# Five split units in layer 1 and LayerNorm sums on GpSimd, in a two-layer transformer kernel

## The chip, the cores and the metric

The kernel runs on one core of a Trainium2 chip. The metric is the device time of one execution in microseconds (us): before the change 2511.05 us, the median of three runs (2510.99 to 2511.12).

The core's engines run their own instruction streams and wait for one another on semaphores. In the profile PE is the matrix engine (PEld its weight loads), DVE the vector engine, ACT the scalar engine with its function tables, POOL the GpSimd engine, and SP the queue from which this kernel issues its DMAs. L1701 is line 1701 of the kernel's file.

## The reference

Two identical layers over 2048 tokens of width 512; A is attention with 32 heads of 16, B a gated FFN of width 1792. The weights are the same in both layers.

```python
def _A_ref(x, wqkv, wo):
    qkv = (x @ wqkv).reshape(B, S, 3, H, Dh) ...
    scores = jnp.einsum("bhqd,bhkd->bhqk", q, k) * (Dh ** -0.5)
    p = _softmax(scores, axis=-1)
    o = jnp.einsum("bhqk,bhkd->bhqd", p, v)
    return o ... @ wo
def _B_ref(x, w_gate, w_up, w_down):
    return (_gelu(x @ w_gate) * (x @ w_up)) @ w_down

x = A_x
x = x + _A_ref(_layernorm(x), A_wqkv, A_wo)
x = x + _B_ref(_layernorm(x), B_w_gate, B_w_up, B_w_down)
x = x + _A_ref(_layernorm(x), A_wqkv, A_wo)
x = x + _B_ref(_layernorm(x), B_w_gate, B_w_up, B_w_down)
```

## The kernel before

**Units.** Attention is cut into units: a block of queries (512 in layer 0; 512, 512, 512, 256, 128 and 128 in layer 1) by a group of four heads. Eight groups make 32 units of 512 queries in layer 0. Every unit goes through two passes. In **pass 1** PE computes scores with queries as rows (L1686), and DVE takes their row maximum over 512 keys, one or two score tiles an instruction (L1701, in `p1_emit`). The maxima of the four blocks of keys are joined on POOL (`fin_pool`, L1062 to L1064), transposed on DVE (L1066) and moved by small DMAs into a spare row of the query tile (`negmax`), so that in **pass 2** PE's scores, now with keys as rows (L1556), come out with the maximum taken off. ACT takes the exponential, again one or two tiles at a time (L1532, in `p2_emit`), PE multiplies by V with a column of ones (L1580), and `nrm` (L1152 on ACT, L1162 and L1167 on POOL) divides. Pass 1 runs ahead of pass 2 by at most six units.

**Folds.** When ACT has time, `f_emit` computes the difference of scores of two blocks of keys (queries times KD, a difference of keys that POOL prepares at L1317), ACT takes its Relu (L1512), and one DVE instruction (L1696) adds the other block's scores and takes the maximum, in place of two tiles of L1701. `want_fold` decides by how far pass 1 is ahead.

**The seam.** Layer 1 needs K and V of all tokens, and those come out of layer 0's last FFN block. So the first six units of layer 1 do pass 1 on the first three of four blocks of keys first, and the first `NSPL` = 3 units also do pass 2 in two parts: part 0 over three blocks of keys with the maximum so far (`fin_part`), kept by ACT in an unused column range of the tile ATT (`part_out`, `keep_part`, L1125); part 1 over the last block, once its K is there. `merge` (L1033, L1036, L1041) scales the kept part and `nrm` adds it on POOL (L1156). All first parts stand ahead of all second parts in the order of units. The last unit of the kernel is split too, with its own place.

**The rest.** `outproj` multiplies by WO and adds to the residual X, `ffn` runs LayerNorm, gate with gelu on ACT (L1262), up and down products; between them, `ln_to_xnt` normalises and transposes tiles of 128 tokens. Its statistics come from `ln_head`: bn_stats and bn_aggr on DVE (L784, L786), then on POOL plus epsilon, power -0.5 and minus the mean (L788, L790, L792) and the normalised tile (L796). It is called as ("mid", layer) ahead of the FFN and as ("in", layer) ahead of the next layer's projections, in groups of up to four tiles. A version on POOL, `ln_pool`, is there and off (`LNP` = 0). Projections, FFN products and the like go through one or two of the eight PSUM banks, and results are taken out by ACT mostly (`pick`).

**The order of the work** is written by a planner in Python while the program is built: it keeps an estimated clock of each engine and at each step chooses between pass 1, pass 2, P times V, the chains of other work (generators that yield what they wait for, each with a due time) and filler matmuls (L1725) that keep PE busy. An engine runs its instructions strictly in the planned order. A chain's step on DVE, ACT or POOL is planned as soon as the estimated times of its operands are near, whatever else that engine has queued. 21 constants of the planner are taken from the rows of `PLAN`, one row for every 16 steps of pass 1 (lead times, how far pass 1 may lead, how much other work at once, how many banks for pairs). Its 129 rows cover the 2048 steps.

The weights lie in SBUF for the whole run; WO is loaded once (`ld_late`). HT holds the FFN's inner activations (14 x 512 columns) and has a lock, `locks["HT"]`, and so has the pair of normalised tiles XN.

## Time and profile before

| | |
|---|---|
| runs, median (lowest, highest) | 2511.05 us (2510.99, 2511.12) |
| the profiled execution: time, span of its instructions | 2511.16 us, 2509.4 us |
| granted TensorE clock | 1.000 |
| busy: PE, DVE, ACT, POOL | 2436.2, 2410.5, 2347.2, 723.2 us |
| row maximum on DVE (L1701), exponential on ACT (L1532) | 2218.8, 2005.3 us |
| bn_stats and bn_aggr of X on DVE (L784, L786) | 47 of each |
| kept first parts (L1125) | 4 |

A group row of the profile reads: line, engine, operation, written tile <- read tiles, shapes, count | busy us, mean ns of one | idle us of the engine just ahead of them, and what ended it. A row of a stretch of time reads: from:to, length, busy us of PE, PEld, DVE, ACT and POOL (with counts), the granted clock, the DMA share and GB/s. A row of the timeline reads: start, us, engine, line, operation. Operations on DVE and ACT overlap a little, so a count times a mean can be above the busy time.

### The profile page before, as it was taken

To read this page: it belongs to the slowest core of one execution; us is meant where nothing else is said; L and a number is where in the kernel's file an instruction comes from. 1 tells how busy PE (TensorE), PEld (TensorE's weight loads), DVE (VectorE), ACT (ScalarE), POOL (GpSimd) and SP (SyncE) were. 2 spreads that over 40 slices of the span, in tenths; PEclk is the share of its full clock that TensorE was granted. 3 is DMA by queue.
4 is the path that set the end of the run, shared out by engine and by line. 5 is a ranking of instruction groups with operands and counts; after the bars stand their busy time and mean duration, and the time that the engine had idled before them with its cause. 6 is when DMAs were issued, how large, how long until landed. Compare 5 with 4: busy or idle time off the path is not lost.

```text
span 2509.4 us, 69489 instructions
## 1 busy us (share of the span) xinstructions
PE 2436.2 (97%) x30346; PEld 1171.7 (47%) x30346; DVE 2410.5 (96%) x3201; ACT 2347.2 (94%) x3293; POOL 723.2 (29%) x1205
## 2 busy tenths in 40 slices
PE   8999999999999999999999999999999999999999
PEld 3444443544444344444434455434553445544655
DVE  8999999999999999999999999999999999999994
ACT  6999999999999999899988699999999999989987
POOL 4112133222312244241144211241213411343431
PEclk9999999999999999999999999999999999999999
DMA  3110000000000000000000000000000000000000
GB/s 95 45 57 6 4 9 2 2 2 9 4 2 2 4 4 6 4 6 2 10 20 2 12 2 2 8 2 10 3 5 6 5 8 2 3 4 11 5 3 11
DMA packets 28225, 25.16 MB, mean 10 GB/s; under 512 B 10768, under 2 KB 26896, under 8 KB 27920
## 3 DMA queue, kind: packets, MB, share of 16 engines
q1 hardware_dynamic: 27920, 20.71, 2.9%
q8 instruction: 238, 3.90, 0.6%
q14 instruction: 67, 0.55, 0.1%
HBM read 9.70 MB, written 2.10 MB: 5 GB/s over the span
## 4 chain that ended last, share of the span: by engine, by line
PE 49%; ACT 31%; DVE 20%; issue 1%; POOL 0%; ACTq 0%; POOLq 0%
ACT SCR L1532 27%; DVE PM L1701 18%; PE PS L1686 16%; PE PS L688 13%; PE PS L1580 11%; PE PS L1556 4%; PE PS L1725 4%; ACT SCR L1512 1%; DVE SCR L1696 1%; PE PS L1505 0%; ACT KT L560 0%; PE PS L850 0%; ACT AO L1180 0%; ACT ATTT L705 0%; ACT XNT L705 0%
## 5 line engine op out<-in xcount | busy, mean ns | idle before, releaser
L1701 DVE TENSOR_REDUCE PM<-PS 128x2 f32<-128x1024 f32 (+1 forms) x2536 | 2218.8, 934 | 51.8 <-PE PS L1556 16.9
L1532 ACT ACTIVATE SCR<-PS 128x1024 bf16<-128x1024 f32 (+1 forms) x2557 | 2005.3, 900 | 58.1 <-PE PS L1556 42.5
L1686 PE MATMUL PS<-KT,QT 32*128 32x512 bf16 x3911 | 1027.7, 385 | 40.2 <-DVE PM L1701 26.5
L1556 PE MATMUL PS<-QT,KT 32*128 32x512 bf16 (+2 forms) x5120 | 916.5, 340 | 3.5 <-ACT SCR L1532 2.6
L1580 PE MATMUL PS<-VP,SCR 128*128 128x51 bf16 (+1 forms) x16384 | 812.4, 188 | 12.5 <-ACT SCR L1532 7.6
L1580 PEld LDWEIGHTS PS<-VP,SCR 128*128 128x128 bf16 x16384 | 574.2, 96 | 491.2 <-issue 406.5
L1686 PEld LDWEIGHTS PS<-KT,QT 32*128 32x128 bf16 x3911 | 245.8, 91 | 526.4 <-DVE PM L1701 290.2
L1725 PE MATMUL PS<-WV,ZER 128*128 128x240 bf16 x2362 | 426.8, 266 | 2.7 <-ACT SCR L1532 2.0
L1162 POOL TENSOR_TENSOR RL<-ACCS,CM 128x16 f32<-128x16 f32 (+2 forms) x71 | 182.7, 2574 | 606.3 <-ACT ACCS L1152 605.6
L1556 PEld LDWEIGHTS PS<-QT,KT 32*128 32x128 bf16 x5120 | 246.9, 91 | 69.5 <-ACT SCR L1532 42.8
L1725 PEld LDWEIGHTS PS<-WV,ZER 128*128 128x128 bf16 x2362 | 177.1, 96 | 66.2 <-issue 52.9
L1280 POOL TENSOR_TENSOR HT<-HT,AO 128x512 bf16<-128x512 bf16 (+1 forms) x106 | 120.9, 1142 | 194.2 <-ACT AO L1278 194.2
L1317 POOL TENSOR_TENSOR KD<-KT 128x512 bf16<-128x512 bf16 x80 | 92.1, 1153 | 220.1 <-PE PS L1505 187.9
L1062 POOL TENSOR_TENSOR PM<-PM 128x16 f32<-128x16 f32 (+3 forms) x146 | 33.3, 228 | 422.7 <-DVE PM L1701 406.9
L688 PE MATMUL PS<-XNT,WU 128*128 128x512 bf16 (+2 forms) x504 | 135.2, 357 | 0.2 <-DVE PM L1696 0.2
L688 PE MATMUL PS<-WD,HT 128*128 128x512 bf16 x448 | 130.3, 380 | 0.0
L1696 DVE CUSTOM_DVE_ANT_0 SCR<-PS,SCR 128x512 bf16<-128x512 f32 x185 | 119.0, 686 | 3.2 <-PE PS L1686 1.0
L688 PE MATMUL PS<-XNT,WG 128*128 128x512 bf16 (+2 forms) x504 | 119.2, 358 | 0.2
L1512 ACT ACTIVATE SCR<-PS 128x512 bf16<-128x512 f32 (+1 forms) x126 | 103.8, 824 | 15.4 <-PE PS L1505 15.1
L1262 ACT ACTIVATE HT<-PS 128x512 bf16<-128x512 f32 (+2 forms) x126 | 68.6, 550 | 38.0 <-PE PS L688 37.5
L1182 POOL TENSOR_TENSOR X<-X,AO 128x512 f32<-128x512 f32 x46 | 58.3, 1268 | 146.8 <-ACT AO L1180 146.8
L1278 ACT ACTIVATE AO<-PS 128x512 f32<-128x512 f32 (+1 forms) x106 | 64.5, 610 | 0.2
(106 smaller groups left out, 1001.0 us busy)
## 6 DMA issues: line engine op xcount, KB each, us to landing
KT<-SG SPq DMA_DIRECT2D x64, 64.0 KB
QT<-MT SPq DMA_DIRECT2D x236, 1.0 KB
...
QT<-MT SPq DMA_DIRECT2D x68, 0.2 KB
```

The costliest lines, as they stand in the source:

```text
L688: ins = e.matmul(out_ap, lhsT=l, rhs=r_, start=(i == 0), stop=(i == n - 1))
L1162: emit("pool", lambda e: e.tensor_tensor(RL[:, s, 0:4 * nq], lsum, CM1[:, 0:4 * nq], op=ALU.pow), r=[("ACCS", s), ("CM1",)], w=[("RL", s)] ...
L1280: emit("pool", lambda e, ft=ft, o=o: e.tensor_tensor(HT[:, ft, c0:c0 + n], HT[:, ft, c0:c0 + n], AO[:, o, 0:n], op=ALU.mult), r=[("AO", o) ...
L1317: emit("pool", lambda e: e.tensor_tensor(KD[:, s, :], KT[:, g, ka * 512:(ka + 1) * 512], KT[:, g, kb * 512:(kb + 1) * 512], op=ALU.subtrac ...
L1512: emit("act", lambda e: e.activation(PT[:, s0:s0 + cnt, :], PS[:, bk:bk + cnt, :], ACTF.Relu), r=bks, w=[("PT", s0 + d) for d in range(cnt ...
L1532: emit("act", lambda e: e.activation(dst, src, ACTF.Exp, scale=DH ** -0.5), r=[BK[bk + i] for i in range(cnt)], w=[("PT", i) for i in slot ...
L1556: ins = e.matmul(bank(bk)[:, i * n:(i + 1) * n], lhsT=KT[32 * j:32 * j + 32, g, kt * 128:(kt + 1) * 128], rhs=QT[32 * j:32 * j + 32, s, 0: ...
L1580: ins = e.matmul(acc, lhsT=PT[:, slot, i * n + qt * 128:i * n + (qt + 1) * 128], rhs=AP(VP, (kt * H + 4 * g + j) * 17, [[NTT * H * 17, 128 ...
L1686: ins = e.matmul(bank(b), lhsT=QT[32 * j:32 * j + 32, s, qt * 128:(qt + 1) * 128], rhs=KT[32 * j:32 * j + 32, g, kb * 512:(kb + 1) * 512], ...
L1696: emit("dve", lambda e, i=i, b=b, sl=sl: e.tensor_tensor_reduce(PT[:, sl, :], bank(b), PT[:, sl, :], 1.0, -3.0e38, ALU.add, ALU.max, po[:, ...
L1701: emit("dve", lambda e: e.tensor_reduce(po, PS[:, bs[0]:bs[0] + cnt, :], axis=AX.X, op=ALU.max), r=bks, w=[("PM", sm) + h[1:] for h in hs] ...
L1725: return e.matmul(PS[:, b, NACC:512], lhsT=ZER[:, :], rhs=WV[:, 0, 0:512 - NACC], start=(b != 7), stop=(b != 7), skip_group_check=True)
```

## The change

- `NSPL` goes from 3 to 5: units 3 and 4 of layer 1 are also done in two parts. Their first parts are kept in the tile of the output weight WO, as 2 x 272 fp32 columns. So part 0 of these two may not begin before layer 0's output projections are all done (`p2_group`), WO is loaded again from memory when both have been merged (`wo_again`), and layer 1's projections wait for that. The last unit's helper slots are shared with unit 0 (`split[u] % NSPL`).
- `ln_pool` is rewritten and takes 20 tiles from `ln_head`: the first eight tiles of ("mid", 0) and of ("in", 1), and the first four of ("mid", 1). It works on four tiles at once: sum by halving in fp32, minus mean, centre, square, sum by halving, power, then the four normalised tiles. Its workspace is eight rows of HT, so that the ("in", 1) groups take HT's lock.
- Room is made: the constant -1 has one column, the statistics one slot, and there is one helper slot less.
- `XL` = 1000 lets `evac` choose DVE when pass 1 leads by over 1000 steps, which the six units don't allow.
- 114 of the 129 rows of `PLAN` are replaced by 117 others, so there are 132; rows behind the 129th are past the last step of pass 1.

```diff
@@ -24,129 +24,132 @@
-    (0.3, 0.1, 0.55, 0.0, 0.0, -0.05, 2, 0, 14, 84, 8, 40, 0.3, 1.0, 0, 2, 2, 2, 5, 2, 0.0),
+    (0.2, 0.1, 0.55, 0.42, 0.3, -0.05, 2, 0, 30, 84, 8, 60, 0.3, 2.0, -5, 2, 4, 3, 7, 1, -0.05),
     (0.2, 0.1, 0.65, 0.62, 0.3, -0.05, 1, 2, 30, 84, 8, 60, 0.3, 1.5, -5, 2, 4, 3, 9, 4, -0.05),
-    (0.3, 0.1, 0.55, 0.42, 0.0, 0.05, 2, 0, 30, 84, 8, 40, 0.3, 2.0, 0, 2, 2, 2, 5, 2, 0.0),
     (0.2, 0.1, 0.55, 0.62, 0.3, -0.05, 1, 2, 30, 84, 8, 60, 0.3, 2.0, -5, 2, 4, 3, 9, 1, -0.05),
-    (0.1, 0.1, 0.55, 0.62, 0.3, -0.05, 1, 2, 30, 84, 8, 60, 0.3, 2.0, -5, 2, 4, 3, 9, 2, -0.05),
...
+    (0.35, 0.1, 0.75, 0.52, 0.3, -0.05, 3, 0, 5, 10, -30, 80, 0.3, 1.5, -5, 2, 1, 3, 5, 1, 0.2),
     (0.1, 0.05, 0.55, 0.42, 0.3, -0.05, 1, 1, 30, 100, 8, 40, 0.5, 2.0, 10, 14, 1, 2, 11, 3, -0.1),
 ]
...
-           NSPL=3, LNP=0, LNT=12
+           NSPL=5, LNT=8, XL=1000
@@ -344,7 +347,7 @@
-        CM1 = sb("CM1", [128, 16], F32)
+        CM1 = sb("CM1", [128, 1], F32)
@@ -359,14 +362,13 @@
-        ST = sb("ST", [128, 4, 6], F32)
+        ST = sb("ST", [128, 1, 6], F32)
-        NSB = NSPL + 1
+        NSB = NSPL
-        LS = sb("LS", [128, 512], F32) if LNP else None
@@ -375,7 +377,7 @@
-        dma_groups = ["ldw_q", "ldw_k", "ldw_v", "ldw_o", "ldw_g", "ldw_u", "ldw_d"]
+        dma_groups = ["ldw_q", "ldw_k", "ldw_v", "ldw_o", "ldw_g", "ldw_u", "ldw_d", "ldw_o2"]
@@ -387,6 +389,8 @@
+        for i in range(3, NSPL):
+            sch.add_alias(("WOP", i - 3), ("WO",))
@@ -699,7 +703,7 @@
-            if pick() == "dve":
+            if fast and pos["p1"] - pos["p2"] > XL or pick() == "dve":
...
@@ -729,61 +733,62 @@
-        def ln_sum(i, xa, xk, first, col, dur):
...
-        def ln_pool(tts, x_of, ready, at):
...
+        def ln_pool(tts, x_of, ready, at, own):
+            n = len(tts)
+            lk = [("HT", r) for r in range(2 * n)]
+            xk = [x_of(tt)[1] for tt in tts]
+            lv = HT[:, 0:2 * n, :].rearrange("p a b -> p (a b)").bitcast(F32).rearrange("p (a b) -> p a b", a=n)
+            xv = X[:, tts[0]:tts[0] + n, :]
+            def tree(w):
+                while w:
+                    yield ("pool", [], [])
+                    emit("pool", lambda e, w=w: e.tensor_tensor(lv[:, :, 0:w], lv[:, :, 0:w], lv[:, :, w:2 * w], op=ALU.add),
+                         r=lk, w=lk, dur=0.18 + n * w / 520.0)
+                    w //= 2
+            for tt in tts:
+                yield ("cond", lambda tt=tt: ready(tt))
+            h = D // 2
+            yield ("pool", xk, lk)
+            emit("pool", lambda e: e.tensor_tensor(lv[:, :, 0:h], xv[:, :, 0:h], xv[:, :, h:D], op=ALU.add),
+                 r=xk, w=lk, dur=0.18 + n * h / 520.0)
+            yield from tree(h // 2)
+            yield ("pool", [], [("LNS", i) for i in range(n)])
+            emit("pool", lambda e: e.tensor_scalar(LNS[:, 2, 0:n], lv[:, :, 0], -1.0 / D, None, op0=ALU.mult),
+                 r=lk, w=[("LNS", i) for i in range(n)], dur=0.24)
+            for i, tt in enumerate(tts):
+                yield ("pool", [], [])
+                emit("pool", lambda e, i=i, tt=tt: e.tensor_scalar(lv[:, i, :], X[:, tt, :], 1.0, LNS[:, 2, i:i + 1], op0=ALU.mult, op1=ALU.add),
+                     r=[xk[i], ("LNS", i)], w=lk[2 * i:2 * i + 2], dur=0.77)
+                yield ("pool", [], [])
+                emit("pool", lambda e, i=i: e.tensor_tensor(lv[:, i, :], lv[:, i, :], lv[:, i, :], op=ALU.mult),
+                     r=lk[2 * i:2 * i + 2], w=lk[2 * i:2 * i + 2], dur=0.18 + D / 520.0)
+            yield from tree(h)
+            yield ("pool", [], [])
+            emit("pool", lambda e: e.tensor_scalar(LNS[:, 0, 0:n], lv[:, :, 0], 1.0 / D, LN_EPS, op0=ALU.mult, op1=ALU.add),
+                 r=lk + [("LNS", i) for i in range(n)], w=[("LNS", i) for i in range(n)], dur=0.24)
+            emit("pool", lambda e: e.tensor_tensor(LNS[:, 1, 0:n], LNS[:, 0, 0:n], CM05[:, 0:n], op=ALU.pow),
+                 r=[("LNS", i) for i in range(n)] + [("CM05",)], w=[("LNS", i) for i in range(n)], dur=0.59 + 0.16 * (n - 1))
+            if not own:
+                locks["HT"] = False
+            for i, tt in enumerate(tts):
+                xa, xki = x_of(tt)
+                yield ("cond", lambda i=i: at["tr"] > i - 2)
+                yield ("pool", [xki, ("LNS", i)], [("XN", i % 2)])
+                emit("pool", lambda e, i=i, xa=xa: e.tensor_scalar(
+                    XN[:, i % 2, :], xa, LNS[:, 2, i:i + 1], LNS[:, 1, i:i + 1], op0=ALU.add, op1=ALU.mult),
+                    r=[xki, ("LNS", i)], w=[("XN", i % 2)], dur=0.77)
+                at["xn"] = i
...
@@ -866,14 +871,18 @@
                                    XNT[:, :, tt * 128:(tt + 1) * 128], [("XNT", tt)])
                     xnt_rec[tt] = tag
                 return
+            by_pool = tag != ("in", 0) and not fast and tts[0] < (LNT - 4 if tag == ("mid", NL - 1) else LNT)
+            if by_pool and tag[0] == "in":
+                yield ("cond", lambda: ready(tts[-1]) and not locks.get("HT") and not locks.get("XN"))
+                locks["HT"] = True
             while locks.get("XN"):
                 yield ("cond", lambda: not locks.get("XN"))
             locks["XN"] = True
-            by_pool = LNP and tag != ("in", 0) and not fast and (tag == ("mid", NL - 1) or tts[0] < LNT)
             if tag == ("in", 0):
                 add(ln_fast(tts, x_of, ready, at, 0.3), due)
             else:
-                add((ln_fast if fast else ln_pool if by_pool else ln_head)(tts, x_of, ready, at), due)
+                own = tag[0] == "mid"
+                add(ln_fast(tts, x_of, ready, at) if fast else ln_pool(tts, x_of, ready, at, own) if by_pool else ln_head(tts, x_of, ready, at), due)
             for i, tt in enumerate(tts):
                 yield ("cond", lambda i=i: at["xn"] >= i)
                 yield ("pe", [("XN", i % 2)], [("XNT", tt)])
...
@@ -997,7 +1006,7 @@
-            i = split[u]
+            i = split[u] % NSPL
...
@@ -1115,6 +1124,9 @@
             i = split[u]
             if i == NSPL:
                 return ATT[:, 2:2 + units[u][3] // 128, 0:136].bitcast(F32), [("ATTX",)]
+            if i >= 3:
+                return (WO[:, :, :].rearrange("p a b -> p (a b)").bitcast(F32)[:, (i - 3) * NACC:(i - 2) * NACC].rearrange("p (a b) -> p a b", a=4),
+                        [("WOP", i - 3)])
             lo = (0, 192, 328)[i]
             return (ATT[:, :, lo:lo + 136].bitcast(F32),
                     [("ATT", g) for g in range(lo // 64, (lo + 135) // 64 + 1)])
@@ -1159,7 +1171,7 @@
-                emit("pool", lambda e: e.tensor_tensor(RL[:, s, 0:4 * nq], lsum, CM1[:, 0:4 * nq], op=ALU.pow),
+                emit("pool", lambda e: e.tensor_tensor(RL[:, s, 0:4 * nq], lsum, AP(CM1, 0, [[1, 128], [0, 4 * nq]]), op=ALU.pow),
@@ -1184,11 +1196,11 @@
-        def outproj(bi):
+        def outproj(bi, again):
-            yield ("cond", lambda: last_u in pv_done)
+            yield ("cond", lambda: last_u in pv_done and (not again or la in wo_rec))
@@ -1319,6 +1331,14 @@
                  r=[("KT", g, ka), ("KT", g, kb)], w=[("KD", s)], dur=1.2)
             kd_rec.add(u)
+        wo_rec = set()
+        def wo_again(la, us):
+            yield ("cond", lambda: all(u in pv_done for u in us))
+            yield ("sp", [], [("WO",)])
+            dma("sp", "ldw_o2", WO[:], wo.rearrange("(a p) n -> p a n", p=128), 0.5, w=[("WO",)])
+            wo_rec.add(la)
         def prep(la, tts, due):
             if la:
                 yield ("cond", lambda: ffn_rec.get(tts[0]) == la - 1)
@@ -1362,7 +1382,10 @@
             for bi, (bl, qi, t0, n) in enumerate(blocks):
                 if bl != la:
                     continue
-                add(outproj(bi), URGENT if bi == len(blocks) - 1 else blk_end[bi] + OPD)
+                late = [u for u in split if u not in extra and units[u][0] == la and split[u] >= 3]
+                if qi == 0 and late:
+                    add(wo_again(la, late), last_p1[u0] + 64)
+                add(outproj(bi, bool(late)), URGENT if bi == len(blocks) - 1 else blk_end[bi] + OPD)
             f0 = 0
             for gi, n in enumerate(ffn_groups[la]):
                 bi = [i for i, b in enumerate(blocks) if b[0] == la and b[2] <= f0 + n - 1 < b[2] + b[3]][0]
@@ -1398,6 +1421,8 @@
             if u >= NU or u not in (part_rec if seq[p2["i"]][1] == 0 else qp2_rec) or gel["on"] is not None:
                 return None
             if seq[p2["i"]][1] == 0 and any(vp_rec.get(kt) != units[u][0] for kt in range(4 * n_part[u])):
+                return None
+            if u in split and u not in extra and split[u] >= 3 and seq[p2["i"]][1] == 0 and any(ao_rec.get(tt) != units[u][0] - 1 for tt in range(NTT)):
                 return None
             if p2["todo"] is None:
                 pt = seq[p2["i"]][1]
```

More of the change, by code (lines that the diff above doesn't have):

```diff
@@ L782, in ln_head @@
                 yield ("cond", lambda tt=tt: ready(tt))
[L783 to L786 removed]
+                yield ("dve", [xk], [("ST", 0)])
+                emit("dve", lambda e, i=i, xa=xa: e.bn_stats(ST[:, 0, :], xa),
+                     r=[xk], w=[("ST", 0)], dur=0.69)
+                emit("dve", lambda e, i=i: e.bn_aggr(MV[:, i, :], ST[:, 0, :]), r=[("ST", 0)], w=[("MV", i)], dur=0.1)
                 yield ("pool", [("MV", i)], [("LNS", i)])
@@ L1012, in fin_rest @@
             nq = units[u][3] // 128
-            i = split[u]
+            i = split[u] % NSPL
             pin = PM[:, s1, 0:nq * 4 * NKB].rearrange("p (a k j) -> p a j k", a=nq, j=4)[:, :, :, NKB - 1]
@@ L1027, in merge @@
             nq = units[u][3] // 128
-            i = split[u]
+            i = split[u] % NSPL
             sgn = (MSEL[:, s1, 0:4 * nq], MSB[:, i, 0:4 * nq]) if u in extra else (MSB[:, i, 0:4 * nq], MSEL[:, s1, 0:4 * nq])
```

48 lines of the change are left out of this document (5 added, 43 removed), and 226 rows, old and new, of the table PLAN.

## The prediction

> **What bounds the kernel now.** I read the page's busy shares first, then the run cut into stages, then the two engines that share the attention work, each shape apart.
>
> ```profile
> span 2509.4 us, 69489 instructions
> PE 2436.2 (97%) x30346; PEld 1171.7 (47%) x30346; DVE 2410.5 (96%) x3201; ACT 2347.2 (94%) x3293; POOL 723.2 (29%) x1205
> ```
>
> Three engines look full. PE's 97% holds filler (L1725, below), so I look at DVE and ACT by stage. The columns are the stretch, its length, and then PE, PEld, DVE, ACT and POOL busy.
>
> ```profile
> 60.00:1260.00 1200.00, 1168.74 (x14405) 552.62 (x14403) 1177.95 (x1590) 1153.34 (x1548) 323.38 (x538) 1.00 0.03 10
> 1260.00:1310.00 50.00, 49.67 (x409) 19.22 (x407) 47.77 (x69) 42.33 (x66) 16.24 (x33) 1.00 0.09 21
> 1310.00:1380.00 70.00, 68.74 (x701) 28.41 (x699) 65.82 (x89) 59.46 (x99) 30.41 (x36) 1.00 0.01 2
> 1380.00:1440.00 60.00, 55.93 (x575) 26.61 (x573) 56.42 (x71) 38.45 (x56) 17.51 (x24) 1.00 0.05 13
> 1440.00:2310.00 870.00, 852.52 (x10899) 409.48 (x10897) 857.06 (x1068) 836.78 (x1184) 244.68 (x388) 1.00 0.02 5
> 2330.00:2460.00 130.00, 126.24 (x2134) 77.31 (x2132) 125.46 (x171) 121.02 (x184) 54.55 (x119) 1.00 0.02 4
> 2460.00:2509.40 49.40, 45.77 (x701) 28.63 (x697) 17.22 (x44) 33.98 (x59) 2.83 (x7) 1.00 0.04 13
> ```
>
> In the long stages DVE is busy 98.2% (1177.95 of 1200) and 98.5% (857.06 of 870), ACT 96.1% and 96.2%: both are nearly full, DVE a little more. The one place with a hole is the seam between the layers, and it is in ACT: from 1380 to 1440 us ACT is idle 60 - 38.45 = 21.55 us, DVE only 3.58. The last 49 us are a chain of the last unit, projection and FFN, in which neither is full.
>
> ```profile
> L1701 DVE TENSOR_REDUCE PM<-PS 128x2 f32<-128x1024 f32 x1190 | 1444.3, 1219 | 42.1 <-PE PS L1556 14.4 <-PE PS L1686 11.8 <-PE PS L1505 0.3
> L1701 DVE TENSOR_REDUCE PM<-PS 128x1 f32<-128x512 f32 x1346 | 904.2, 682 | 9.7 <-PE PS L1556 2.4 <-PE PS L1686 1.4
> L1696 DVE CUSTOM_DVE_ANT_0 SCR<-PS,SCR 128x512 bf16<-128x512 f32 x185 | 119.0, 686 | 3.2 <-PE PS L1686 1.0 <-PE PS L1556 0.8 <-PE PS L1505 0.2
> L784 DVE BATCH_NORM_STATS2 ST<-X 128x6 f32<-128x512 f32 x47 | 32.1, 684 | 0.0
> L1696 DVE DVE_READ_ACCUMULATOR2_ANT PM<- 128x1 f32 x185 | 15.4, 83 | 0.0
> L786 DVE BATCH_NORM_AGGREGATE MV<-ST 128x2 f32<-128x6 f32 x47 | 8.6, 182 | 1.6
> ```
>
> ```profile
> L1532 ACT ACTIVATE SCR<-PS 128x1024 bf16<-128x1024 f32 x1539 | 1478.1, 1083 | 44.6 <-PE PS L1556 34.8 <-PE PS L1686 1.7 <-DVE PM L1701 1.0
> L1532 ACT ACTIVATE SCR<-PS 128x512 bf16<-128x512 f32 x1018 | 570.3, 624 | 13.5 <-PE PS L1556 7.7 <-PE PS L1686 0.2
> L1512 ACT ACTIVATE SCR<-PS 128x1024 bf16<-128x1024 f32 x59 | 63.5, 1077 | 1.8 <-PE PS L1505 1.6
> L1512 ACT ACTIVATE SCR<-PS 128x512 bf16<-128x512 f32 x67 | 40.3, 601 | 13.6 <-PE PS L1505 13.5
> L1725 PE MATMUL PS<-WV,ZER 128*128 128x240 bf16 x2362 | 426.8, 266 | 2.7 <-ACT SCR L1532 2.0 <-ACT ACCS L1152 0.6
> ```
>
> (The last row is a PE row of the same view.) L1701 is the row maximum of pass 1 on DVE, L1532 the exponential of pass 2 on ACT. They are tied by the **fold** (L1512 on ACT, L1696 on DVE): it takes two score tiles of pass 1 for one DVE instruction. A fold costs ACT (63.5 + 40.3) / 185 = 0.56 us and costs DVE 0.686 + 0.083 = 0.77 in place of one two-tile reduction of 1.219: DVE gains 0.45. So time freed on either engine is passed to the other by doing fewer or more folds. **One microsecond freed on DVE alone shortens a stage by 0.56 / (0.56 + 0.45) = 0.55; one freed on ACT alone by 0.45.** PE's 426.8 us of filler show that PE isn't the limit over the whole, though from 1260 to 1380 it is close (49.67 of 50, 68.74 of 70).
>
> **The change part by part.**
>
> *LayerNorm of 20 tiles to POOL.* The condition takes the first two groups of four tiles of (mid, layer 0) and (in, layer 1) and the first of (mid, layer 1): 16 tiles before the seam, 4 behind it. DVE loses 0.684 + 0.182 = 0.866 us a tile: 13.9 us before the seam, 3.5 behind, 17.3 together. POOL takes over sums, centring and squares:
>
> ```profile
> L1182 POOL TENSOR_TENSOR X<-X,AO 128x512 f32<-128x512 f32 x46 | 58.3, 1268 | 146.8 <-ACT AO L1180 146.8
> L1156 POOL TENSOR_TENSOR ACCS<-ACCS,ATT 128x272 f32<-128x272 f32 x3 | 2.3, 757 | 8.1 <-ACT ACCS L1152 8.1
> L1062 POOL TENSOR_TENSOR PM<-PM 128x16 f32<-128x16 f32 x61 | 13.5, 221 | 40.3 <-DVE PM L1701 36.1
> L796 POOL TENSOR_SCALAR XN<-X,LNS 128x512 bf16<-128x512 f32 x47 | 36.1, 768 | 3.2 <-POOL LNS L792 1.1 <-PE PS L1556 0.2
> L788 POOL TENSOR_SCALAR LNS<-MV 128x1 f32<-128x1 f32 x47 | 10.4, 222 | 44.3 <-DVE MV L786 42.5
> L790 POOL TENSOR_TENSOR LNS<-LNS,CM 128x1 f32<-128x1 f32 x47 | 26.9, 572 | 3.9
> L792 POOL TENSOR_SCALAR LNS<-MV 128x1 f32<-128x1 f32 x47 | 11.3, 239 | 4.1
> L836 POOL TENSOR_TENSOR ACCS<-ACCS,CM 128x4 f32<-128x4 f32 x2 | 2.0, 1021 | 0.2
> ```
>
> 512 elements take 1.268 and 272 take 0.757, so 2.13 ns an element and 0.18 fixed. For a group of four: first add of 1024 elements 2.36; eight halvings from 512 down to 4 elements, 1.27 + 0.73 + 0.45 + 0.32 + 0.25 + 0.22 + 0.20 + 0.20 = 3.64; scale 0.24; four centrings of 0.77 and four squares of 1.27, 8.15; the tree again from 1024, 6.00; scale and power 0.24 + 1.02. Sum **21.65 us in one piece**, for the planner lets no other POOL work in between (its steps ask for nothing that isn't there). Five groups: 108 us; off go 20 x (0.222 + 0.572 + 0.239) = 20.7. POOL rises by about 88 us to 810 of 2500, no bound; what the piece delays is a rival below. That POOL's load slows DVE is excluded by two stretches with POOL busy 19.85 and 40.62 of 100 us, in which the two-tile reduction takes the same:
>
> ```profile
> 1800.00:1900.00 100.00, 97.48 (x1330) 49.74 (x1328) 98.75 (x127) 99.34 (x124) 19.85 (x30) 1.00 0.02 5
> 1900.00:2000.00 100.00, 98.88 (x1010) 40.00 (x1008) 98.38 (x134) 93.40 (x144) 40.62 (x69) 1.00 0.02 5
> ...
> L1701 DVE TENSOR_REDUCE PM<-PS 128x2 f32<-128x1024 f32 x48 | 58.6, 1222 | 1.1 <-PE PS L1556 0.6
> ...
> L1701 DVE TENSOR_REDUCE PM<-PS 128x2 f32<-128x1024 f32 x54 | 65.0, 1218 | 0.9
> ```
>
> *Five units in two parts.* Before the last block of keys of layer 1 is there, ACT can work only on first parts of split units. ACT's rows in order of time show the last of the three kept (L1125), and then nothing until merging begins (L1036):
>
> ```profile
> 1388.57 0.40 ACT L1125 ACTIVATE ATT<-PS 128x272 f32<-128x272 f32 x1
> ...
> 1390.29 0.60 ACT L705 ACTIVATE SG<-PS 128x512 bf16<-128x512 f32 x1 [0.69 <-PE PS L688]
> 1393.43 0.60 ACT L705 ACTIVATE SG<-PS 128x512 bf16<-128x512 f32 x1 [2.54 <-PE PS L688]
> 1399.73 0.22 ACT L1036 ACTIVATE DW<-DW 128x16 f32<-128x16 f32 x1 [5.70 <-POOL DW L1033]
> ```
>
> A first part is 4 heads x 12 key tiles = 48 tiles = 24 double exponentials of 1.083: 26 us. Two more give 52 us of work, more than the 21.55 idle from 1380 to 1440, and PE has filler to give up there. I take the hole as filled: ACT gains 21.55, less two more keeps of 0.40 and factors of 0.22, so 20.3. DVE pays for two more units a small reduction, two small elementwise steps and a second transpose; no row is quoted for them, the nearest of so few columns is L786 with 0.182: four of these are 0.73 a unit, 1.5 for both. POOL's merge and add, two steps of 272 elements at 0.757 (L1156), lie in its 60 - 17.51 = 42.5 idle us of that stage.
>
> *Output weight reloaded.* One DMA of 512 KB on SP's queue, behind the maxima's and queries' moves, after units 3 and 4 are merged; the same load took 3.8 us:
>
> ```profile
> WO<-in_A_wo_dram SPq DMA_DIRECT2D x1, 512.0 KB, 3.8
> ```
>
> The first projection of layer 1 needs it only when its eight units are through, three units or 3 x 32 double exponentials of 1.083, 104 us, later. Cost nothing; uncovered it would be these 3.8. The other new wait, for layer 0's projections ahead of units 3 and 4, is met by then: the last keys of layer 1 come out of the last FFN, which itself waits for those projections, and first parts of units 3 and 4 begin only behind the third keep at 1388.57. Smaller tiles (statistics, the minus-one constant) reuse a slot in DVE's own order: nothing.
>
> *Constants.* 114 of 129 rows of the plan change. They decide, among others, how many reductions and exponentials run on one tile. Two singles instead of a double cost DVE 2 x 0.682 - 1.219 = 0.145 and ACT 2 x 0.624 - 1.083 = 0.165. If a tenth of the singles (1346 and 1018) were paired or split, that is 67 x 0.145 = 9.8 and 51 x 0.165 = 8.4. No row says in which direction; I take nothing and keep 10 us on both sides.
>
> **Sum**, against the profiled execution's 2511.16 us (span 2509.4; median of the runs 2511.05, so no correction): before the seam 13.9 x 0.55 = -7.7; seam 20.3 x 0.45 = -9.1 on ACT and +1.5 x 0.55 = +0.8 on DVE; behind it 3.5 x 0.55 = -1.9. Together -17.9: **2493.3 us**. Were there no exchange and DVE the only bound, it would be 17.3 - 1.5 = -15.8; the two ways lie close together.
>
> **The rivals.**
>
> *The POOL piece starves ACT (slower).* A unit's pass 2 needs its maximum, which POOL finishes. Around the second group the maximum comes (L1066) only a little ahead of the end of the unit in front (L1152):
>
> ```profile
> 604.95 0.21 DVE L1066 STREAM_TRANSPOSE MT<-MSEL 128x32 bf16<-128x32 bf16 x1
> ...
> 611.60 0.41 ACT L1152 ACTIVATE ACCS<-PS 128x272 f32<-128x272 f32 x1
> ```
>
> Slack 6.65 us. With a POOL piece of 21.65 in front of it, the maximum can be 21.65 late and ACT stand 15 us. If that happens in four of the five groups, ACT loses 60, less what folds fill; at 0.45 that is 27 us, and the sum is -17.9 + 27 = +9: **2520**. It decides from 40 us of ACT lost (40 x 0.45 = 17.9). For it: the slack of 6.65, and POOL's strict order. Against it: the piece is shorter than a unit's stretch (32 x 1.083 = 35 us), so it can miss the maximum; and folds can fill such gaps, as long as their key differences, also POOL's, are there. The Trainium skill, GPSIMD Engine Reference, section 3.1, gives GpSimd about 2.6 cycles an element where VectorE needs about one and says that elementwise work belongs on VectorE; the slope above, 2.13 ns, bears out the price, and by the rule this edit should lose, which is this rival. I give it 0.11.
>
> *The hole isn't filled, or ACT's gain finds no taker.* The first parts of units 3 and 4 come late, or PE, full until 1380, holds them. Then only LayerNorm counts: -7.7 - 1.9 + 0.8 = -8.8: **2502**. This is also the case in which the split doesn't do what it says. For it: PE's rows from 1260 to 1380. Against: the filler after 1380. 0.20.
>
> *The constants pair more tiles.* 10 us more: **2483**. For it: 1346 single reductions, a third of DVE's tiles; against: singles stand where a bank is lent to other matmuls, and that need stays. 0.17.
>
> **How the numbers follow.** Forecast 2493 (2487 to 2499) 0.45; the rivals 0.11, 0.20 and 0.17; nothing left over, gains and the POOL price cancelling, 0.07. About 0.2%, 5 us, is what a measurement of this kernel can tell from no change. Faster: 0.45 + 0.20 + 0.17 = 0.82; same 0.07; slower 0.11. The range takes 2483 less the same again for the constants at its lower end, 2473, and reaches above to 2514, short of the slower rival; about 0.08 lies below and 0.10 above.
>
> **What would show it.** LayerNorm right: 27 rows of bn_stats on X instead of 47, DVE busy near 2395 or fewer folds. Seam right: five keeps, ACT over 55 of 60 us from 1380 to 1440 by its equivalent place, and folds or an earlier end behind it. POOL right: pieces of about 22 us, with no idle of ACT of over 5 us beside them; idle ahead of L1532 well over the 58 us of its two rows would say that the maximum came late. Constants: the counts of the two forms of L1701. The prediction is wrong if DVE's and ACT's busy times fall and the span doesn't.

## The result, and the profile after

The changed kernel takes **2492.04 us**, the median of four runs (2491.92 to 2492.15), against 2511.06 (2510.99 to 2511.12) for the kernel before: 19.0 us less, a ratio of 0.9924 with an interval of [0.9907, 0.9941]. The forecast was 2493.3. The total is right; the experiments show that the terms behind it are not all right.

The head of the page of the kernel after, then its stretches of time (columns as before: stretch, length, PE, PEld, DVE, ACT, POOL):

```profile
span 2490.2 us, 69394 instructions
PE 2416.1 (97%) x30236; PEld 1163.3 (47%) x30236; DVE 2397.1 (96%) x3163; ACT 2350.7 (94%) x3413; POOL 800.9 (32%) x1274
```

```profile
60.00:1260.00 1200.00, 1167.95 (x14453) 555.38 (x14452) 1178.55 (x1526) 1153.78 (x1638) 392.48 (x597) 1.00 0.04 10
1310.00:1380.00 70.00, 69.18 (x772) 29.56 (x770) 63.60 (x86) 65.79 (x116) 26.21 (x33) 1.00 0.01 2
1380.00:1440.00 60.00, 57.40 (x750) 27.75 (x750) 56.96 (x81) 57.95 (x79) 7.37 (x11) 1.00 0.05 11
```

The hole is gone: ACT is idle 60 - 57.95 = 2.05 us from 1380 to 1440, where it was 21.55. But in the long stretch ahead of the seam nothing has moved: DVE is busy 1178.55 us of 1200 there, and it was 1177.95 with 13.9 us more of LayerNorm to do.

The groups of DVE and ACT, each shape apart (L1726 is the row maximum, L1721 the fold, L789 bn_stats, L1557 the exponential):

```profile
L1726 DVE TENSOR_REDUCE PM<-PS 128x2 f32<-128x1024 f32 x1207 | 1459.5, 1217 | 38.2 <-PE PS L1581 19.9 <-PE PS L1711 7.4 <-PE PS L1530 0.4
L1726 DVE TENSOR_REDUCE PM<-PS 128x1 f32<-128x512 f32 x1314 | 882.9, 681 | 13.9 <-PE PS L1581 6.9 <-PE PS L1711 1.7
L1721 DVE CUSTOM_DVE_ANT_0 SCR<-PS,SCR 128x512 bf16<-128x512 f32 x184 | 118.7, 686 | 2.6 <-PE PS L1711 0.7 <-PE PS L1581 0.4
L789 DVE BATCH_NORM_STATS2 ST<-X 128x6 f32<-128x512 f32 x27 | 18.4, 683 | 0.0
```

```profile
L1557 ACT ACTIVATE SCR<-PS 128x1024 bf16<-128x1024 f32 x1409 | 1351.2, 1074 | 25.6 <-PE PS L1581 17.9 <-DVE PM L1726 0.5 <-PE PS L1711 0.2
L1557 ACT ACTIVATE SCR<-PS 128x512 bf16<-128x512 f32 x1278 | 701.5, 623 | 17.7 <-PE PS L1581 10.8
```

20 bn_stats fewer, as planned; 184 folds where 185 were, so over the whole run nothing was exchanged by their number. ACT's idle time ahead of its exponentials is 25.6 + 17.7 = 43.3 us (58.1 before): no sign of late maxima.

To see where the 19 us arise I cut both runs at the same steps of pass 1: counting L1701 and L1726 as one step for two tiles and half a step for one, and a fold as one, pass 1 has 2048 steps. The stretches end at steps 1024, 1216, 1408 and 1600; the last row runs from step 2047, one short of the end of pass 1, to the end. Before:

```profile
0.00:1205.10 1205.10, 1164.00 (x13974) 546.12 (x13975) 1174.59 (x1608) 1142.96 (x1547) 340.03 (x571) 1.00 0.05 14
1205.10:1449.70 244.60, 237.66 (x2499) 104.98 (x2498) 233.81 (x311) 203.38 (x306) 77.81 (x116) 1.00 0.05 11
1449.70:1676.70 227.00, 221.64 (x2809) 107.56 (x2808) 223.88 (x286) 219.68 (x287) 60.35 (x97) 1.00 0.02 4
1676.70:1909.60 232.90, 227.98 (x3040) 112.38 (x3038) 230.00 (x288) 229.57 (x313) 56.54 (x83) 1.00 0.02 6
...
2463.90:2509.40 45.50, 42.25 (x634) 26.48 (x634) 13.43 (x38) 30.38 (x53) 1.91 (x6) 1.00 0.04 14
```

After:

```profile
0.00:1202.60 1202.60, 1160.78 (x13955) 545.11 (x13956) 1172.72 (x1540) 1141.03 (x1649) 406.35 (x627) 1.00 0.06 15
1202.60:1452.70 250.10, 243.48 (x2822) 111.57 (x2822) 237.86 (x323) 231.96 (x336) 73.28 (x103) 1.00 0.03 7
1452.70:1664.90 212.20, 205.28 (x2551) 97.77 (x2547) 209.70 (x287) 204.22 (x265) 76.35 (x123) 1.00 0.03 8
1664.90:1892.00 227.10, 222.12 (x2870) 107.76 (x2870) 224.37 (x291) 222.49 (x328) 62.62 (x89) 1.00 0.02 5
...
2448.90:2490.20 41.30, 38.35 (x566) 24.21 (x563) 15.02 (x40) 26.65 (x50) 1.62 (x5) 1.00 0.05 15
```

Second column, after less before: ahead of the seam -2.5; the seam itself +5.5; the two stretches behind it -14.8 and -5.8; the last -4.2. (Between steps 1600 and 2047, +2.6.) So the seam gets longer for DVE while ACT's idle time in it falls from 41.2 to 18.1 us, and the gain stands behind it. What ACT did with the time can be counted: in the seam it takes the exponentials of 398 score tiles, 320 in before, and between steps 1216 and 1600 it has 776 left to do, 856 in before. How ACT's gain became DVE's shows in the folds between steps 1216 and 1600, first before, then after:

```profile
L1696 DVE CUSTOM_DVE_ANT_0 SCR<-PS,SCR 128x512 bf16<-128x512 f32 x19 | 12.1, 686 | 0.1
```

```profile
L1721 DVE CUSTOM_DVE_ANT_0 SCR<-PS,SCR 128x512 bf16<-128x512 f32 x45 | 29.1, 686 | 0.8 <-PE PS L1581 0.3
```

26 more, at 0.45 us of DVE saved by each: 11.7 us. Ahead of step 1024 it is the other way; folds and bn_stats, before and after:

```profile
L1696 DVE CUSTOM_DVE_ANT_0 SCR<-PS,SCR 128x512 bf16<-128x512 f32 x138 | 89.0, 686 | 2.7 <-PE PS L1686 1.0 <-PE PS L1556 0.5 <-PE PS L1505 0.2
L784 DVE BATCH_NORM_STATS2 ST<-X 128x6 f32<-128x512 f32 x24 | 16.4, 684 | 0.0
```

```profile
L1721 DVE CUSTOM_DVE_ANT_0 SCR<-PS,SCR 128x512 bf16<-128x512 f32 x113 | 72.9, 687 | 1.5 <-PE PS L1711 0.4 <-PE PS L1581 0.2
L789 DVE BATCH_NORM_STATS2 ST<-X 128x6 f32<-128x512 f32 x8 | 5.5, 682 | 0.0
```

25 folds fewer: of 13.9 us freed on DVE, 25 x 0.45 = 11.2 are given back. What ACT got for it does not show as free time. Its exponentials up to step 1024, before and after:

```profile
L1532 ACT ACTIVATE SCR<-PS 128x1024 bf16<-128x1024 f32 x772 | 744.8, 1071 | 16.4 <-PE PS L1556 11.4 <-DVE PM L1701 1.0
L1532 ACT ACTIVATE SCR<-PS 128x512 bf16<-128x512 f32 x404 | 228.8, 618 | 3.9 <-PE PS L1556 2.5
```

```profile
L1557 ACT ACTIVATE SCR<-PS 128x1024 bf16<-128x1024 f32 x663 | 636.3, 1074 | 11.6 <-PE PS L1581 8.4 <-DVE PM L1726 0.5
L1557 ACT ACTIVATE SCR<-PS 128x512 bf16<-128x512 f32 x618 | 338.8, 627 | 6.9 <-PE PS L1581 3.9
```

The Relus on two tiles fall by 13.0 us there (59.3 to 46.3). Against that, 214 more exponentials run on one tile, and all of them together keep ACT busy for 961.2 us, 955.8 in before, at nearly the same work (1944 tiles and 1948); and ACT takes out nine more results of projections before step 1024, 5.7 us. So its busy time is only 1.9 us shorter.

ACT's timeline has the fourth and fifth kept part (L1137, into WO); the others stand at 1315.1, 1345.5 and 1373.8. POOL's has one piece of LayerNorm:

```profile
1404.80 0.39 ACT L1137 ACTIVATE WO<-PS 128x272 f32<-128x272 f32 x1
1428.67 0.44 ACT L1137 ACTIVATE WO<-PS 128x272 f32<-128x272 f32 x1
```

```profile
598.44 2.35 POOL L754 TENSOR_TENSOR HT<-X 128x1024 f32<-128x1024 f32 x1
...
606.28 1.04 POOL L765 TENSOR_TENSOR HT<-HT 128x512 f32<-128x512 f32 x1
...
619.81 1.04 POOL L771 TENSOR_TENSOR LNS<-LNS,CM 128x4 f32<-128x4 f32 x1
```

From 598.44 to 620.85 it is 22.4 us in one piece (estimate 21.65). The reload of WO is issued at 1467.6 and takes 3.7 us; the first product with it starts at 1580.7.

### The profile page after: what moved, and what is told of

Its sections match the earlier page's. It is cut to its first block, busy times and chain, and to the rows that moved or that the text cites. A ratio compares the mean times of both kernels' runs of the same rounds, so it can differ in the third digit from the quotient of the medians.

```text
span 2490.2 us, 69394 instructions
## 1 busy us (share of the span) xinstructions
PE 2416.1 (97%) x30236; PEld 1163.3 (47%) x30236; DVE 2397.1 (96%) x3163; ACT 2350.7 (94%) x3413; POOL 800.9 (32%) x1274
## 4 chain that ended last, share of the span: by engine, by line
PE 47%; DVE 28%; ACT 23%; issue 1%; DMA 0%; SPq 0%; ACTq 0%
DVE PM L1726 26%; ACT SCR L1557 21%; PE PS L1711 15%; PE PS L692 13%; PE PS L1605 10%; PE PS L1581 4%; PE PS L1750 4%; DVE SCR L1721 1%; ACT SCR L1537 1%; PE PS L855 1%; PE PS L1530 0%; ACT AO L1192 0%; ACT XNT L709 0%; ACT SG L709 0%; ACT ATTT L709 0%
## 5 line engine op out<-in xcount | busy, mean ns | idle before, releaser
L1726 DVE TENSOR_REDUCE PM<-PS 128x2 f32<-128x1024 f32 (+1 forms) x2521 | 2212.5, 938 | 52.1 <-PE PS L1581 26.8
L1557 ACT ACTIVATE SCR<-PS 128x1024 bf16<-128x1024 f32 (+1 forms) x2687 | 2015.6, 859 | 43.3 <-PE PS L1581 28.6
L1711 PE MATMUL PS<-KT,QT 32*128 32x512 bf16 x3912 | 1019.1, 384 | 42.1 <-DVE PM L1726 26.1
L1581 PE MATMUL PS<-QT,KT 32*128 32x512 bf16 (+2 forms) x5120 | 926.1, 340 | 2.4 <-ACT SCR L1557 1.7
L1605 PE MATMUL PS<-VP,SCR 128*128 128x51 bf16 (+1 forms) x16384 | 803.3, 187 | 10.8 <-ACT SCR L1557 7.1
L1750 PE MATMUL PS<-WV,ZER 128*128 128x240 bf16 x2252 | 412.4, 266 | 4.6 <-ACT SCR L1557 3.5
L1750 PEld LDWEIGHTS PS<-WV,ZER 128*128 128x128 bf16 x2252 | 170.3, 96 | 59.4 <-issue 43.6
L1292 POOL TENSOR_TENSOR HT<-HT,AO 128x512 bf16<-128x512 bf16 x98 | 113.8, 1163 | 186.8 <-ACT AO L1290 186.7
L1721 DVE CUSTOM_DVE_ANT_0 SCR<-PS,SCR 128x512 bf16<-128x512 f32 x184 | 118.7, 686 | 2.6 <-PE PS L1711 0.7
L1537 ACT ACTIVATE SCR<-PS 128x1024 bf16<-128x1024 f32 (+1 forms) x123 | 102.9, 836 | 18.6 <-PE PS L1530 18.3
L692 PEld LDWEIGHTS PS<-XNT,WG 128*128 128x128 bf16 x504 | 37.5, 97 | 55.1 <-issue 30.1
```

Of the source, the lines that this page charges most:

```text
L692: ins = e.matmul(out_ap, lhsT=l, rhs=r_, start=(i == 0), stop=(i == n - 1))
L1292: emit("pool", lambda e, ft=ft, o=o: e.tensor_tensor(HT[:, ft, c0:c0 + n], HT[:, ft, c0:c0 + n], AO[:, o, 0:n], op=ALU.mult), r=[("AO", o) ...
L1537: emit("act", lambda e: e.activation(PT[:, s0:s0 + cnt, :], PS[:, bk:bk + cnt, :], ACTF.Relu), r=bks, w=[("PT", s0 + d) for d in range(cnt ...
L1557: emit("act", lambda e: e.activation(dst, src, ACTF.Exp, scale=DH ** -0.5), r=[BK[bk + i] for i in range(cnt)], w=[("PT", i) for i in slot ...
L1581: ins = e.matmul(bank(bk)[:, i * n:(i + 1) * n], lhsT=KT[32 * j:32 * j + 32, g, kt * 128:(kt + 1) * 128], rhs=QT[32 * j:32 * j + 32, s, 0: ...
L1605: ins = e.matmul(acc, lhsT=PT[:, slot, i * n + qt * 128:i * n + (qt + 1) * 128], rhs=AP(VP, (kt * H + 4 * g + j) * 17, [[NTT * H * 17, 128 ...
```

## The experiments

Two theories were tested. **By terms**: each part frees time of its own, folds carry it between ACT and DVE at 0.55 and 0.45, and the new constants are a detail. **By the order**: the constants are the order of the work; a part is worth something only in an order made for it, and what an engine gains is kept only where the other has time to match. Runs of the kernel before beside these had medians between 2511.1 and 2511.3.

### The parts in the orders that were there

e1 has LayerNorm on POOL alone, e2 the split alone and e4 both, all with the rows of before; e3 has the new rows alone.

```diff
-NSPL=5 ... LNT=8      PLAN of after
+NSPL=3 ... LNT=8      PLAN of before     (e1)
+NSPL=5 ... LNT=0      PLAN of before     (e2)
+NSPL=3 ... LNT=0      PLAN of after      (e3)
+NSPL=5 ... LNT=8      PLAN of before     (e4)
```

> Only the LayerNorm sums on POOL; three split units and the plan rows of before. Theory (freed DVE time is shared with ACT through the folds): the sum's own part, -7.7 before the seam and -1.9 behind it, so 2501.5 us. Rival (what is freed ahead of the seam is lost at the seam, since the keys of layer 1's last block come at the same 1400 us in before and after): only the 3.5 us behind the seam count, 2508 to 2510. Rival (POOL's piece of 22 us starves ACT where the rows of the plan don't fit it): 2513 or more, with idle ahead of the exponentials above the 58 us of before.

> Only the five split units with the reloaded output weight; LayerNorm statistics on DVE and the plan rows of before. Theory: ACT's idle time from pass 1 step 1024 to 1216, 40.8 us in before and 18.0 in after, falls by about 20 and comes back at 0.45: -8.3, so 2502.8 us. Rival (ACT's time is worth its full size, since behind the seam ACT is what lags): -15 to -20, 2491 to 2496. Rival (it finds no taker without the new rows): 2508 to 2514.

> Only the new plan rows; three split units, LayerNorm statistics on DVE. Theory (constants zero, 10 us on both sides): 2511, with the counts of single-tile exponentials raised as in after (1278 for 1018). Rival (the new rows carry a good part of the gain by themselves): under 2504. Rival (rows and order of work belong together, and rows chosen for another order do harm): over 2516.

> LayerNorm sums on POOL and five split units, with the plan rows of before. Theory (the two parts add, the rows give nothing): -17.9, 2493 us. Rival (rows carry it): 2503 or more. If single-tile exponentials ahead of the seam, 404 in before and 618 in after up to step 1024, come from the rows, they are near 404 here, there are more folds, and it could be below 2492.

All four are slower than before: e1 2593.36 (1.0328 [1.0298, 1.0358]), e2 2560.52 (1.0197 [1.0167, 1.0226]), e3 2543.29 (1.0128 [1.0099, 1.0158]), e4 2599.40 (1.0352 [1.0322, 1.0382]). Nothing like a sum of small terms, then; but they say little about the parts. e1, e2 and e4 lose most of it at one place where the order no longer fits. e1 is 6.4 us ahead of before at step 512, and at step 1088 64 us behind (e4 67): PE is full of other products, pass 1 of layer 1 begins late and DVE stands idle,

```profile
1240.00:1280.00 40.00, 40.00 (x410) 17.05 (x410) 8.61 (x15) 36.07 (x71) 7.24 (x13) 1.00 0.00 1
```

busy 8.61 of 40 us; it takes out the results of projections one by one and waits for each. In e2 ACT is busy 229.8 of 250 us in the seam (203.4 of 244.6 in before) and the folds of the stretch behind it go from 13 to 31, so the seam's mechanism is there without the other parts; the kernel is level with before up to step 1856 (+0.5 us) and loses 46 us behind it, where PE is again full of other work and DVE waits for products of the FFN; then PE's granted clock falls too (0.83):

```profile
2260.00:2300.00 40.00, 40.00 (x489) 19.01 (x486) 4.15 (x6) 37.46 (x74) 4.10 (x4) 1.00 0.01 2
2300.00:2340.00 40.00, 37.45 (x252) 17.22 (x252) 21.08 (x31) 11.47 (x18) 4.32 (x14) 0.83 0.07 19
```

e3 has no such place: it is 21.5 us behind already at step 1024, with DVE busy 1188.9 of 1226.5 us, all the statistics still on it and 109 folds where before has 138. One thing these runs do settle: up to step 1024 there are 404 exponentials on one tile in before, 413 in e1 and e4, and 688 in e3. The rows make them, not the parts.

### The parts, each with rows made for it

In e9 to e11 the rows of PLAN were changed at random, some 1200, 1100 and 700 times, and a change was kept when the planner's own estimate of the end fell. e12 does the same to the kernel after, 600 times. Where the searches began shows in the rows' numbers: of the 2709 in e9, 2178 stand at the same place in after's rows (1193 in before's); of e10's, 1919 stand in before's (1403 in after's); e11 starts from e9.

```diff
+NSPL=3 LNT=8  rows made anew             (e9)
+NSPL=5 LNT=0  rows made anew             (e10)
+NSPL=5 LNT=8  rows made anew from e9's   (e11)
+NSPL=5 LNT=8  rows of after, made further (e12)
```

> As the first run (LayerNorm sums on POOL, three split units), but with plan rows chosen anew for this order of work: some 1200 random changes of rows, kept where the planner's own estimate of the end fell. Theory (the part has a value of its own once rows fit): 9.6 us under before, 2501.5. Rival (DVE time freed ahead of the seam alone is lost at the seam): within 4 us of 2511. The estimate stood 11 to 14 us under before's and after's measured times; by that, 2498.0 becomes 2509 to 2512.

> As the second run (five split units, statistics on DVE), rows chosen anew, some 1100 changes. Theory: 8.3 us under before, 2502.8. Rival (it needs the DVE time that LayerNorm frees): within 4 us of 2511. The estimate, 2496.2, becomes 2507 to 2510.

> Both parts, rows chosen anew from those of the LayerNorm-only kernel, not from after's, some 700 changes: the control for the last two. If it comes clearly below both of them with fewer changes, the two parts are worth more together than apart, and the difference isn't only how long rows were fitted. The estimate, 2489.3, becomes 2500 to 2503. Rival (all of after's gain is longer fitting of rows): 2507 or more.

> After with some 600 further changes of its rows, estimate 2478.8 for 2479.9. If after's rows were short of fitted, there would be several us left; theory: 1 us, 2490 to 2492.

e9: 2510.12 (0.9995 [0.9985, 1.0006]), 1.0 us less than before. e10: 2508.48 (0.9989 [0.9979, 0.9999]), 2.7 less. e11: 2500.55 (0.9957 [0.9941, 0.9972]), 10.6 less. e12: 2492.23 (0.9924 [0.9907, 0.9940]), as after.

The seam's stretch, cut at steps 1024 and 1216, in e9, e10 and e11:

```profile
1203.00:1451.00 248.00, 240.50 (x2574) 109.67 (x2592) 235.75 (x317) 203.17 (x292) 78.45 (x114) 1.00 0.03 7
```

```profile
1205.00:1457.00 252.00, 244.45 (x2759) 111.60 (x2784) 236.69 (x323) 232.55 (x340) 71.90 (x105) 1.00 0.05 11
```

```profile
1203.00:1453.00 250.00, 242.32 (x2783) 111.28 (x2805) 238.06 (x323) 230.36 (x332) 72.89 (x104) 1.00 0.03 7
```

Without the split (e9) ACT keeps its hole (203.17 busy of 248), and behind it there are 18 folds between steps 1216 and 1600 and no gain: pass 1 is 1.0 us late at 1216 and 0.9 late at 1600. With the split (e10, e11) ACT is busy 232.55 and 230.36, 38 or 39 folds stand behind the seam, and pass 1 gains 11.3 and 12.0 us by step 1600, after losing 7.9 and 5.5 in the seam.

So the seam's chain is borne out: hole filled, folds, DVE. LayerNorm alone is worth 1.0 us and the split alone 2.7; together they are worth 10.6. The split on top of LayerNorm is 9.6 (e9 and e11, rows of one origin; 700 further changes of rows are in it, but 600 further ones in e12 brought nothing). LayerNorm on top of the split would be 2508.48 - 2500.55 = 7.9, but e10's rows come from before's and e11's in the end from after's, so this is not LayerNorm's alone. As measured, the parts don't add; how much of that is the rows' is open. And the rows are a term of their own: e11 and after differ in nothing else, keep within 0.5 us of each other up to step 1216, and then part by 8.5 us up to step 1600. In those stretches the kernel after has 32 + 13 folds, e11 28 + 10.

### What DVE time costs in a fixed order

e5 and e6 keep the order of the kernel after, instruction by instruction, and add 16 pairs of bn_stats and bn_aggr whose results nobody uses: four in each of the four groups ahead of the seam (e5), or all 16 in the group behind it (e6).

```diff
+            ln_cnt["n"] += 1
+            if ln_cnt["n"] < 5:                      # e6: == 5
+                for i, tt in list(enumerate(tts)) * 1:   # e6: * 4
+                    sch.op("dve", lambda e, tt=tt: e.bn_stats(ST[:, 0, :], X[:, tt, :]), ...)
+                    sch.op("dve", lambda e, i=i: e.bn_aggr(MV[:, i, :], ST[:, 0, :]), ...)
```

> The order of after, unchanged, with the statistics of the 16 tiles ahead of the seam put back on DVE as well (16 bn_stats and bn_aggr, results unused: 13.9 us of DVE). With the order fixed nothing can be handed to ACT. Theory (DVE time counts fully, ahead of the seam too): +10 to +14 on 2492, so 2502 to 2506. Rival (the seam takes it up, as the gain of before to after at pass 1 step 1024 is only 2.5 us): under +4, below 2496.

> The order of after, unchanged, with 16 bn_stats and bn_aggr (13.9 us of DVE, results unused) at the one POOL group behind the seam. Theory (behind the seam DVE is the bound): +12 to +14, 2504 to 2506. Rival (ACT is what limits there): under +6, with DVE's idle time smaller by the rest.

e5: 2512.25, 20.2 us more than after (1.0003 [0.9992, 1.0014] to before). e6: 2507.83, 15.8 more (0.9985 [0.9974, 0.9997]); its 16 pairs stand in a row from 1596.8 to 1611.8 us. The 13.9 us of work cost more than themselves at both places, and pass 1 and the end move together by as much. In e6 the 16 pairs hold DVE for 15.0 us, which is nearly all of the 15.8. So the ratio of 0.55 isn't a property of the kernel; it can hold only where the planner is free to trade folds.

Why more than 13.9 in e5: its rows at one group, and the stretch that follows, in e5 and in after.

```profile
373.71 0.68 DVE L776 BATCH_NORM_STATS2 ST<-X 128x6 f32<-128x512 f32 x1
374.43 0.18 DVE L777 BATCH_NORM_AGGREGATE MV<-ST 128x2 f32<-128x6 f32 x1
374.64 0.69 DVE L776 BATCH_NORM_STATS2 ST<-X 128x6 f32<-128x512 f32 x1
...
377.37 1.79 DVE L1731 TENSOR_REDUCE PM<-PS 128x2 f32<-128x1024 f32 x2
```

```profile
372.00:378.00 6.00, 2.95 (x45) 1.47 (x40) 5.76 (x12) 3.64 (x4) 5.50 (x9) 0.97 0.01 3
378.00:384.00 6.00, 5.38 (x56) 2.68 (x56) 4.91 (x7) 3.97 (x4) 5.17 (x12) 0.50 0.01 2
```

```profile
372.00:378.00 6.00, 5.80 (x87) 2.93 (x83) 5.96 (x9) 5.97 (x7) 5.50 (x9) 1.00 0.02 3
378.00:384.00 6.00, 5.12 (x73) 2.57 (x71) 5.83 (x7) 6.00 (x8) 5.17 (x12) 1.00 0.01 2
```

The four pairs hold DVE for 377.37 - 373.71 = 3.66 us. PE, whose banks are not emptied meanwhile, stands idle for 3.54 us until DVE's next maximum (375.08 to 378.62) and falls from 5.80 to 2.95 us busy, and in the next 6 us its granted clock is 0.50: 56 matmuls take 5.38 us where 73 took 5.12, and DVE waits for scores. A group costs 20.2 / 4 = 5.05 us in the mean. At the other three groups PE stands idle for 3.40 to 3.52 us, and its clock is 0.50 for 6.8 us each time. The Trainium skill, TensorE: Matmul & The Clock Gate, "What's actually happening", says that the clock falls to half after an idle window of about 3.4 us and comes back after a busy one; the 3.40 to 3.54 us of idle time and the 0.50 behind them agree.

### POOL's piece, longer and shorter

e7 does the first add of each piece six times. e8 sums only the first 64 of 512 columns, so that a piece takes 10.4 us. The order is that of after in both.

```diff
+            for _ in range(5):                        # e7
+                sch.op("pool", lambda e: e.tensor_tensor(lv[:, :, 0:h], xv[:, :, 0:h], xv[:, :, h:D], op=ALU.add), ...)
-            ... lv[:, :, 0:h], xv[:, :, 0:h], xv[:, :, h:D]      # e8
+            ... lv[:, :, 0:32], xv[:, :, 0:32], xv[:, :, 32:64]
```

> The order of after, unchanged, the first addition of each POOL group done six times: each piece longer by 5 x 2.35 = 11.8 us, 59 us more POOL in all. Theory (POOL isn't a bound, maxima come in time behind a gelu phase): 0 to +3. Rival (a piece in front of a unit's maximum starves ACT): four groups of up to 11.8, +15 to +47, with idle ahead of the exponentials above after's 43 us.

> The order of after, unchanged; the statistics are taken from the first 64 of 512 columns only, so that a POOL piece falls from 22.4 us to about 9. Theory (the piece costs nothing where it stands): 0 to -1. Rival (it delays maxima already): -5 or more.

e8: 2492.09 (0.9922 [0.9893, 0.9951]), the same as after to 0.05 us: where it stands, the piece of 22.4 us costs nothing. e7: 2552.25 (1.0161 [1.0132, 1.0191]), 60 us more for five times 11.8 = 59 us on POOL; pass 1 falls behind that of after by 12.8, 10.0, 12.9, 9.2 and 14.0 us at the five pieces. The first place in e7, then the same in after, and what ACT waited for there in e7:

```profile
370.00:430.00 60.00, 51.97 (x626) 25.09 (x623) 48.22 (x68) 47.92 (x58) 44.00 (x58) 0.85 0.01 2
```

```profile
370.00:430.00 60.00, 57.32 (x694) 27.11 (x690) 58.91 (x84) 56.76 (x73) 36.18 (x63) 1.00 0.02 4
```

```profile
414.57 0.60 ACT L709 ACTIVATE XNT<-PS 128x512 bf16<-128x512 bf16 x1 [6.10 <-PE PS L857]
```

DVE loses 10.7 us there and ACT 8.8, with POOL at 44 of 60. ACT waits for the transpose of a normalised tile (L857), which PE does as soon as POOL has written the tile, behind the sums and the steps queued after them:

```profile
413.10 0.77 POOL L781 TENSOR_SCALAR XN<-X,LNS 128x512 bf16<-128x512 f32 x1
```

At the last piece it is a normalised tile too (DVE waits 6.78 us for the transpose). At the second, third and fourth it is the maximum: its transposition stands next in DVE's order, and DVE waits for POOL,

```profile
653.08 0.21 DVE L1077 STREAM_TRANSPOSE MT<-MSEL 128x32 bf16<-128x32 bf16 x1 [8.66 <-POOL MSEL L1075]
735.35 0.21 DVE L1077 STREAM_TRANSPOSE MT<-MSEL 128x32 bf16<-128x32 bf16 x1 [5.13 <-POOL MSEL L1075]
967.85 0.21 DVE L1077 STREAM_TRANSPOSE MT<-MSEL 128x32 bf16<-128x32 bf16 x1 [6.44 <-POOL MSEL L1075]
```

and over the whole run ACT is idle 42.1 + 37.1 = 79.2 us ahead of its exponentials, 43.3 in after. How much room there was can be read in after: ahead of these three maxima POOL stands idle for 0.69, 5.24 and 5.10 us, and the transposition comes 2.64, 1.58 and 0.45 us after the maximum is ready. That makes 3.3, 6.8 and 5.6 us; 11.8 less these is 8.5, 5.0 and 6.2, which is what DVE waits. The cost is higher than the wait (10.0, 12.9 and 9.2), and at all five places PE runs at a granted clock of 0.50 behind it, for 10 to 27 us (from 732.4 to 759.7 at the third). That the clock makes up the difference is argued, not tested.

So the rival's mechanism is real: a late maximum, as the prediction said, at three pieces, and a late normalised tile at two, with DVE starved as well as ACT. What counts is whether somebody waits at the end of the piece: the 22.4 us are placed where nobody does, with 3 to 7 us to spare at the three maxima.

## Why the prediction was right, and where it was not

The forecast was -17.9 and the measurement -19.0. By place: ahead of the seam -7.7 forecast and -2.5 measured; seam and behind it up to step 1600 -9.1 + 0.8 - 1.9 = -10.2 forecast and 5.5 - 20.6 = -15.1 measured; from there nothing forecast, and +2.6 and then -4.2 in the last stretch measured.

*The seam: right in mechanism, and in size beside LayerNorm.* ACT's idle time fell by 19.5 us in the 60 us named (20.3 forecast); it came back as 26 folds, 11.7 us of DVE, where 9.1 was written. e9 shows that without the split neither the folds nor the gain appear, and e11 against e9 prices the split at 9.6; forecast were 9.1 - 0.8 = 8.3. Without LayerNorm on POOL it gave 2.7 (e10).

*DVE's price in the seam: mis-sized.* Small operations were put at 0.73 us a unit, 1.5 in all and 0.8 in the sum. The five that a split unit needs take 0.99, so 2.0 in all. But pass 1 loses 5.5 us in that stretch in after and 7.9 in e10: in after there are also 3 folds fewer (7, 10 in before), more maxima on one tile and 1.45 us more idle time on DVE, which the sum left out. e9, which has 7 folds there too and no split, loses 2.8.

*LayerNorm ahead of the seam: this step failed.* "13.9 x 0.55 = -7.7" assumed that time freed on DVE is exchanged for ACT time and kept. The exchange took place, 25 folds fewer, but ACT's busy time up to step 1024 fell only from 1142.96 to 1141.03 (exponentials on one tile and projections taken out earlier used up what the Relus left), and pass 1 is 2.5 us ahead at step 1024. ACT's part of the first merge, which waits for the last keys, stands at 1399.73 us in before and 1399.89 in after. The price of DVE time is not small: e5 shows that putting it back in this order costs 20.2. But freeing it, alone and with rows of its own, gives 1.0 (e9). Why the planner can't use it ahead of the seam was not settled: PE is full from 1310 to 1380 (69.18 of 70), which may be what holds the keys back, and no run here relieved PE there. Late keys can't be all of it, for in e9 that merge stands at 1394.63, 5 us sooner, and pass 1 is 1.0 us late at step 1216 all the same.

*The constants: not nothing.* They were put at 0 within 10 us, by the pairing of tiles. Rows alone are worth 8.5 us between e11 and after, at the edge of the bound, and not by pairing on DVE: single maxima went from 1346 to 1314, 16 pairs or 2.3 us, and single exponentials went up, from 1018 to 1278. The prediction's price for that was too high as well: 107 pairs split up to step 1024 would be 17.7 us at 0.165, and all exponentials together rose by 5.4. A price taken from mean lengths leaves out that instructions overlap: 772 x 1.071 is 827 us, and those instructions were busy for 744.8. What after has over e11 are 7 folds and less idle time behind the seam. With rows that don't fit the loss is 32 to 88 us (e1 to e4), far outside the bounds of 10; nothing in the profile of before told the one case from the other.

*POOL.* The piece was estimated at 21.65 and took 22.4; it costs nothing (e8). The slack it has at three maxima is 3.3 to 6.8 us (e7), so the rival was near.

*The output weight.* That it costs nothing was right: the reload is issued at 1467.6 and its tile first used at 1580.7, 113 us of cover where 104 were reckoned.

*The last stretch* was left out. From step 2047 on, pass 2 has 5 double exponentials fewer to do (16 after, 21 before), and the end follows 4.2 us sooner. So the sum came out right because LayerNorm's missing 5.2 us and the seam's price were made up by rows and tail, which is luck; of the forecast's gains only the seam's is borne out.
